# Seven instead of 6.1 conversion steps in every expert slot of an attention and mixture-of-experts kernel

## The chip, the cores and the metric

The kernel runs on one core of a Trainium2 chip. The metric is the device time of one launch in microseconds (us), taken as the median of several runs. The engines are called as in the profile: PE (TensorE, matmuls), ACT (ScalarE), DVE (VectorE), POOL (GpSimd) and SP (SyncE, which issues most of the DMAs). Each engine works through its own queue in program order.

## The reference

```
attn = softmax(scale * q @ k.T + bias(log-distance MLP)) @ v     # 4 x 8 heads, 576 positions, depth 64
x    = attn as [2304 tokens, 512]
e    = argmax(normalised x @ normalised expert_emb)              # 8 experts, one for each token
x    = gate * (relu(x @ w1[e]) @ w2[e])                          # 512 -> 1024 -> 512
out  = (relu(x @ w_in) ** 2) @ w_out                             # 512 -> 2048 -> 512, weights in float64
```

## The kernel before

The program has three stages: the attention, the expert stage and a last dense feed-forward. PE multiplies everything as pairs of 16-bit halves (a high and a low part, three products for each pair), so weights and tokens are split into two halves first.

**Expert stage.** Tokens that share an expert are gathered into slots of 128 rows. `run_slots` (line 1300) runs 22 slots, t = 0 to 21, one after the other. Slot t does, in program order: the first half of the next slot's first product (`ff1(t+1, 0)`), the split of half the first weights of slot t+2 into w1b (`split_w1(t+2, 0)`), the transposition of slot t+2's tokens (`x_T`), the split of slot t+3's tokens (`x_split`), the second half `ff1(t+1, 1)` with `split_w1(t+2, 1)`, the second product `ff2(t)`, its copy-out, and the loads of slot t+4's first weights (`load_slot`). While `ff2(t)` runs, SP issues the four quarters of slot t+1's second weights into the buffers that PE leaves (`load_w2`, line 1020; the profile calls the buffers vt and the source wsc). The weights' loads and splits are conditional: they move data only where a slot's expert differs from that of the slot before. In the traced run that is so for slots 3, 6, 7, 9, 10, 12, 13 and 16.

**The conversion.** Beside this the stage turns the last feed-forward's float64 weights into the halves, in 16 pieces of 1 MB (`convert`, line 1113): pieces 0 to 7 are w_in (into wih, in SBUF), pieces 8 to 15 are w_out (stored to DRAM as wosc). The generator `pieces` cuts the work into 121 steps. Two of them begin it (four loads, L1128 of piece 0), and then come seven for each n from 0 to 16:

```
1  DVE  L1130, L1131 of piece n        (n = 1 to 8: SP also loads piece n+3, L1118 or L1121)
2  ACT  high half of piece n-1         (L1141 or L1152)
3  DVE  L1133 of piece n
4  DVE  low half of piece n-1          (L1143 or L1154; n = 10 to 13: SP also loads piece n+2)
5  DVE  L1135 of piece n
6  POOL L1148 of piece n (w_out only); ACT L1128 of piece n+1
7  SP   store of piece n-1 (w_out only, L1156)
```

Four buffers (wr in the profile) hold raw pieces, two (tb) hold pieces in work. `run_slots` calls `piece(t, n)` at four places of slot t: n = 0 behind `split_w1(t+2, 0)`, n = 1 behind `split_w1(t+2, 1)` and so ahead of `ff2(t)` and its weight loads, n = 2 and n = 3 behind the copy-out of `ff2(t)`. The pace is a constant:

```
def piece(t, n):
    while done[0] < (1 if t < 2 else 1 + (t - 2 + 0.25 * n) * CPACE):
        next(conv, None)
        done[0] += 1
```

At the end of slots 11 to 14 `halves(us, DVE)` and `y_rows` (lines 1050, 1272 and 1274) add the split of four row blocks of the result for the last stage.

**Last stage.** From the end of the slots PE runs the products of the dense feed-forward without a break: `g_unit` (line 1435, weights wih) and `ff2_of` (line 1473, weights woh, loaded from wosc at line 1529).

Of the kernel before, what the change touches and what calls it, by code (L numbers as in the profile page):

```python
# [39 lines left out]
W1S, W2S, YS = 64.0, 64.0, 2.0 ** -8  # L40
WIS, RS, WOS = 64.0, 2.0 ** -8, 64.0
OUTS = 2.0 ** -22
CPACE = 6.1
NCONV, NWIN = 16, 8
HSW = 134
TINY64, HUGE = 2.0 ** -15 * 1.125, 3e38
# [38 lines left out]
def body(ctx: ExitStack, tc: tile.TileContext, q, k, v, wsm, emb, tau, mw1, mw2, win, wout, cst_d, lsk_d, ids_d, out):  # L85
# [873 lines left out]
    with tc.manual_schedule():  # L959
# [331 lines left out]
# [4 lines that stand above are left out]
# [319 lines left out]
```

## Time and profile before

| | |
|---|---|
| runs | 1007.3, 1009.07 and 1011.41 us, median 1009.07 |
| profiled execution | 1002.49 us, span 1000.6 us |
| mean clock granted to TensorE | 0.981 of full speed |
| PE matmuls busy | 945.9 us (95%) |
| DVE, ACT, POOL busy | 652.2, 540.8, 517.8 us (65%, 54%, 52%) |
| slots, first `ff2` to the last stage's first matmul | 398.87 to 642.19 us of the span |

PE is busy nearly all the time, so what counts is where it stands still, in which stage, and what it then waits for. The other engines and the DMA queue matter only where PE waits for them.

### The profile page before, as it was taken

The numbers are of one execution on the slowest core, as the hardware profiler recorded it, in microseconds if no ns is written. First come the engines' busy times: TensorE is split into PE (matmuls) and PEld (weight loads), VectorE is DVE, ScalarE is ACT, GpSimd is POOL, SyncE is SP. The second block draws the span as 40 slices with busy tenths as digits, with TensorE's granted clock in tenths as the row PEclk, the third lists the DMA queues.
The fourth block names the chain that finished last, engine by engine and source line by source line (L and its number), as shares of the span: only waits on it lengthen the run. The fifth ranks groups of instructions, "written<-read, shape, count | busy, mean of one in ns | idle before, by whom it ended". The sixth has DMA issues, their size and how long they took to land. (4 is left out here: it accounts for less than half of the span.)

```text
span 1000.6 us, 25069 instructions
## 1 busy us (share of the span) xinstructions
PE 945.9 (95%) x9725; PEld 750.9 (75%) x9725; DVE 652.2 (65%) x1260; ACT 540.8 (54%) x1000; POOL 517.8 (52%) x509
## 2 busy tenths in 40 slices
PE   8687999999999879999989999999999999999998
PEld 5355676677677658777657766688888888888887
DVE  6665797887988765588966977335455546364442
ACT  5576676877877674456746664355233324324231
POOL 1212548356735362466637787476455645454651
PEclk9799999999999989999999999999999999999999
DMA  8989895998879432698898674371111120111101
GB/s 289 297 259 306 263 302 193 266 293 289 239 248 332 156 132 97 247 340 316 324 407 305 214 296 161 119 315 43 33 54 34 36 59 17 49 44 32 33 1 43
DMA packets 79260, 187.18 MB, mean 187 GB/s; under 512 B 26680, under 2 KB 27320, under 8 KB 76544
## 3 DMA queue, kind: packets, MB, share of 16 engines
q1 hardware_dynamic: 73232, 170.50, 50.8%
q0 software_dynamic: 5904, 15.02, 4.3%
q8 instruction: 78, 1.28, 0.5%
q14 instruction: 46, 0.38, 0.1%
HBM read 171.65 MB, written 51.73 MB: 223 GB/s over the span
## 5 line engine op out<-in xcount | busy, mean ns | idle before, releaser
L1451 POOL TENSOR_TENSOR gf<-gf 128x256 f32<-128x256 f32 x144 | 166.2, 1174 | 144.9 <-DVE gf L1448 124.2
L1435 PE MATMUL pf<-big,wih 128*128 128x256 f16 x1728 | 196.0, 273 | 0.9 <-PEq L1389 0.9
L1435 PEld LDWEIGHTS <-wih 128*128 128x128 f16 x1728 | 169.0, 98 | 20.9 <-issue 1.3
L1473 PEld LDWEIGHTS <-g 128*128 128x128 f16 x1512 | 147.4, 98 | 18.7 <-issue 1.0
L1441 ACT ACTIVATE gf<-pf 128x512 f32<-128x512 f32 x72 | 42.3, 597 | 192.8 <-PE pf L1435 131.4
L475 POOL TENSOR_TENSOR wh<-wr,w2s_c 128x256 f16<-128x256 f32 x128 | 82.9, 679 | 116.6 <-DMA wr<-in_mw_dram 59.3
L1232 PE MATMUL ph<-x,w1b 128*128 128x128 f16 x2112 | 125.1, 219 | 2.5 <-ACT x L1216 1.7
L1232 PEld LDWEIGHTS <-w1b 128*128 128x128 f16 x2112 | 120.5, 98 | 6.9 <-issue 1.9
L1247 PE MATMUL py<-vt,h 128*128 128x512 f16 x528 | 119.2, 383 | 5.7 <-DMA vt<-wsc 5.7
L526 ACT ACTIVATE pr<-ssb,mn 128x576 f32<-128x576 f32 x144 | 111.7, 776 | 8.6 <-DVE mn L513 8.6
L1459 DVE TENSOR_TENSOR g<-gf,g 128x1792 f16<-128x1792 f32 x36 | 85.5, 2375 | 46.5 <-ACT g L1458 46.5
L513 DVE CUSTOM_DVE_ANT_0 ssb<-ps_s,bias 128x576 f32<-128x576 f32 x144 | 107.4, 748 | 6.1 <-DMA bias<-bias_d 5.1
L1448 DVE TENSOR_TENSOR gf<-gf 128x1024 f32<-128x1024 f32 x28 | 34.3, 1225 | 114.2 <-ACT gf L1441 114.2
L502 PE MATMUL ps_s<-kst,qd 128*128 128x288 f16 (+1 forms) x640 | 97.5, 293 | 8.7 <-DVE mn L513 7.2
L1247 PEld LDWEIGHTS <-h 128*128 128x128 f16 x528 | 51.1, 98 | 64.8 <-issue 8.6
L535 PE MATMUL ps_t<-cst,pr 128*128 128x128 f32 x576 | 92.3, 283 | 0.7 <-DVE pt L212 0.4
L560 PE MATMUL pv<-pt,vt 128*64 128x128 f32 (+1 forms) x1280 | 85.7, 277 | 6.8 <-DMA vt<-in_v_dram 5.9
L560 PEld LDWEIGHTS pv<-pt,vt 128*64 128x64 f32 x1280 | 68.0, 142 | 23.7 <-issue 17.3
L535 PEld LDWEIGHTS ps_t<-cst,pr 128*128 128x128 f32 x576 | 64.9, 144 | 23.2 <-issue 19.3
L502 PEld LDWEIGHTS <-qd 128*128 128x128 f16 (+1 forms) x640 | 56.7, 102 | 23.2 <-issue 12.9
L210 ACT COPY pt<-ps_t 128x512 f32<-128x512 f32 x99 | 57.1, 576 | 10.8 <-PE ps_t L535 10.8
L1458 ACT CAST g<-gf 128x1792 f16<-128x1792 f32 x36 | 60.3, 1676 | 4.4 <-POOL gf L1451 4.4
(199 smaller groups left out, 1537.9 us busy)
## 6 DMA issues: line engine op xcount, KB each, us to landing
vt<-wsc SPq DMA_DIRECT2D x88, 512.0 KB
wr<-in_mw_dram SPq DMA_DIRECT2D x76, 512.0 KB
kst<-in_mw_dram SPq DMA_DIRECT2D x44, 512.0 KB
wsc<-wh SPq DMA_DIRECT2D x32, 512.0 KB
bias<-bias_d SPq DMA_DIRECT2D x16, 576.0 KB
bias_d<-rt SPq DMA_DIRECT2D x28, 295.5 KB
qd<-qh SPq DMA_DIRECT2D x64, 128.0 KB
wr<-in_win_dram SPq DMA_DIRECT2D x8, 1024.0 KB
```

The lines of the kernel that those rows point to most:

```text
L475: POOL.tensor_tensor(out=wh[:, 0, n:n + 256], in0=wr[:, n:n + 256], in1=w2s_c.to_broadcast([P, 256]), op=ALU.mult)
L502: PE.matmul(s[r, hf, :288], lhsT=qd[:, h2, i, pr, r], rhs=kst[x - x % 2][:, pr, h2, x % 2, js], start=(i == 0), stop=(i == 1))
L513: DVE.tensor_tensor_reduce(out=ss.rearrange("p (a j) -> p a j", a=2), in0=s[:, :, :288], in1=btile[bkey[u]][:, h2].rearrange("p (a j) -> p ...
L526: ACT.activation(pr_sb[k_ // 2][:, h2], ssb.pop(k_), AF.Exp, bias=mns.pop(k_), scale=-1.0, accum_out=sums[c, b][:, h:h + 1])
L535: PE.transpose(pt_ps[k_][:, jc * P:(jc + 1) * P], src[:, j0:j0 + P], eye)
L560: PE.matmul(pv[o, cs], lhsT=vb[:, 2 * jc + h2, d] if jc < 4 else vb[o, 8, d], rhs=a[h2][:, jc, cs] if jc < 4 else e[o, cs], start=(jc == 0 ...
L1232: PE.matmul(p_[:, f4, :], lhsT=w[:, a, kc, f * P:(f + 1) * P], rhs=x2[:, b, kc, :], start=(i == 0), stop=(i == 11))
L1247: PE.matmul(p_, lhsT=h2[:, a, fc, :], rhs=wb2[fc // 2][:, b, fc % 2, :], start=(i == 0), stop=(i == 23))
L1435: PE.matmul(p_[:, h], lhsT=wih[:, a, kc, f * P:(f + 1) * P], rhs=y2[:, b, kc, :], start=(i == 0), stop=(i == 11))
L1451: POOL.tensor_tensor(out=g[:, d], in0=g[:, x], in1=g[:, y], op=op)
L1459: DVE.tensor_tensor(out=gt[:, 1, :, c:c + 2, :], in0=g[:, 1:8], in1=gt[:, 0, :, c:c + 2, :], op=ALU.subtract)
L1473: PE.matmul(ps, lhsT=gt[:, a, s, c, :], rhs=woh[:, c, b, w, :], start=(i == 0 and first), stop=(i == 23 and end), skip_group_check=True)
```

## The change

The pace of the conversion goes from 6.1 to 7 steps a slot.

```diff
-CPACE = 6.1
+CPACE = 7.0
```

With 7.0 the call at n = 0 of every slot from 3 on runs step 6 of a piece, n = 1 runs steps 7 and 1, and n = 2 and n = 3 together, behind `ff2(t)`, run steps 2 to 5. The last step comes in slot 19, where with 6.1 it comes in slot 21. No instruction's size changes.

SP's queue in slot 6, from the end of `load_slot(9)` over the store of slot 5's rows (y_d) to the first quarter of slot 7's second weights (vt from wsc), before:

```order
L1011 DMA kst_105<-in_mw_dram 128x1024
L1263 DMA y_d<-ys 128x514
L1020 ISA
L1020 DMA vt_106<-wsc_65 128x2048
L1036 UNCONDITIONAL_BRANCH
```

And the same place now:

```order
L1011 DMA kst_105<-in_mw_dram 128x1024
L1263 DMA y_d<-ys 128x514
L1118 DMA wr_7791<-in_win_dram 128x2048
L1036 UNCONDITIONAL_BRANCH
L1020 ISA
L1020 DMA vt_106<-wsc_65 128x2048
```

In each of slots 3 to 10 a conversion load of 1 MB (L1118 or L1121) stands ahead of the slot's weight loads now. Before, the loads of slots 3, 4 and 5 stood behind the second weights and ahead of the first, slot 6 had none, and those of slots 7 to 10 already stood ahead.

DVE's queue at the turn from slot 14 to slot 15, from the second pair of weight splits for slot 16 (L1027) to the low half of slot 16's first hidden rows (the L1238 at the end), before:

```order
L1027 SCALAR_TENSOR_TENSOR w1b<-wr_5262,w1b 128x2x512 x2
L1036 UNCONDITIONAL_BRANCH x2
L1031 TENSOR_LOAD ne_i
L1154 SCALAR_TENSOR_TENSOR wr_8433<-tb,wr_8433 128x1792
L1256 COPY ys<-ga 128x2
L1135 SCALAR_TENSOR_TENSOR tb<-wr_8655,tb 128x1024
L1050 TENSOR_TENSOR xs<-us_78,xs 128x512
L1272 COPY meta<-us_78 128x2
L1274 CAST orow<-us_78 128x1
L1001 SCALAR_TENSOR_TENSOR zid<-ti 128x1
L1002 TENSOR_TENSOR yidx<-yidx,zid 128x1
L1238 SCALAR_TENSOR_TENSOR h_9651<-ph,h_9651 128x512
```

And now, from right behind the same pair of splits:

```order
L1130 TENSOR_SCALAR tb<-tb 128x1024
L1131 TENSOR_SCALAR tb<-tb 128x1024
L1256 COPY ys<-ga 128x2
L1133 SCALAR_TENSOR_TENSOR tb<-wr_9148,tb 128x1024
L1154 SCALAR_TENSOR_TENSOR wr_8665<-tb,wr_8665 128x1792
L1135 SCALAR_TENSOR_TENSOR tb<-wr_9148,tb 128x1024
L1050 TENSOR_TENSOR xs<-us_78,xs 128x512
L1272 COPY meta<-us_78 128x2
L1274 CAST orow<-us_78 128x1
L1001 SCALAR_TENSOR_TENSOR zid<-ti 128x1
L1002 TENSOR_TENSOR yidx<-yidx,zid 128x1
L1238 SCALAR_TENSOR_TENSOR h_9674<-ph,h_9674 128x512
```

All five DVE instructions of a piece stand between the splits and the hidden rows now, where before L1130, L1131 and L1133 stood elsewhere.

## Rows read from the trace of the kernel before

**Rows 1.** Windows: us; PE, PEld, DVE, ACT, POOL busy; clock, DMA share, GB/s

```profile
400.00:642.00 242.00, 233.31 (x2628) 168.94 (x2626) 181.26 (x268) 138.69 (x172) 157.91 (x137) 0.99 0.75 277
...
642.00:998.00 356.00, 354.08 (x3240) 316.36 (x3240) 167.51 (x160) 126.34 (x158) 182.86 (x161) 1.00 0.19 59
```

**Rows 2.** What PE waited for from 395 to 650: us, times, longest

```profile
PE py L1247 <- DMA vt<-wsc: 5.7, 3, 4.2
PE ph L1232 <- ACT x L1216: 1.0, 1, 1.0
PE pf L1435 <- PEq L1389: 0.9, 1, 0.9
PE ph L1232 <- DVE w1b L1027: 0.8, 2, 0.6
PE px L1215 <- POOL xs L1050: 0.4, 1, 0.4
```

**Rows 3.** PE's timeline, slots 6, 7, 10, 16: start, us, what, idle before

```profile
462.10 2.84 PE L1232 MATMUL ph<-x,w1b 128*128 128x128 f16 x48
...
477.29 5.34 PE L1247 MATMUL py<-vt,h 128*128 128x512 f16 x24 [1.35 <-DMA vt<-wsc]
...
514.94 7.03 PE L1247 MATMUL py<-vt,h 128*128 128x512 f16 x24 [4.17 <-DMA vt<-wsc]
...
580.91 2.84 PE L1232 MATMUL ph<-x,w1b 128*128 128x128 f16 x48 [1.04 <-ACT x L1216]
```

**Rows 4.** Windows of the slot stage, columns as in rows 1

```profile
454.00:456.00 2.00, 2.00 (x11) 0.92 (x10) 2.00 (x3) 2.00 (x4) 1.02 (x1) 1.00 0.47 141
456.00:462.00 6.00, 6.00 (x70) 4.34 (x69) 6.00 (x6) 3.05 (x5) 5.76 (x4) 1.00 0.84 300
462.00:478.00 16.00, 14.64 (x185) 11.34 (x183) 11.45 (x19) 10.07 (x13) 8.32 (x7) 1.00 0.99 361
478.00:488.00 10.00, 10.00 (x122) 7.53 (x121) 8.75 (x12) 6.01 (x9) 6.76 (x5) 1.00 1.02 406
488.00:494.00 6.00, 6.00 (x42) 3.16 (x40) 5.78 (x7) 5.97 (x8) 3.41 (x3) 1.00 0.31 82
...
516.00:518.00 2.00, 2.00 (x6) 0.76 (x5) 2.00 (x3) 0.09 (x1) 0.88 (x1) 0.50 1.02 412
```

**Rows 5.** The page's DMA issues: the conversion's loads of pieces 0 to 7

```profile
wr<-in_win_dram SPq DMA_DIRECT2D x8, 1024.0 KB
```

**Rows 6.** SP's timeline, slots 5 and 6: start, us, issues

```profile
455.29 4.22 SPq L1020 DMA_DIRECT2D vt<-wsc  x4
462.07 0.34 SPq L1118 DMA_DIRECT2D wr<-in_win_dram  x1
464.02 2.63 SPq L1011 DMA_DIRECT2D kst<-in_mw_dram  x4
...
467.83 2.74 SPq L1020 DMA_DIRECT2D vt<-wsc  x4
```

**Rows 7.** DVE's timeline, slots 5, 14 and 15: start, us, what

```profile
457.60 3.31 DVE L1027 SCALAR_TENSOR_TENSOR w1b<-kst,w1b 128x1024 f16<-128x1024 f32 x2
460.83 1.21 DVE L1135 SCALAR_TENSOR_TENSOR tb<-wr,tb 128x1024 uint32<-128x1024 uint32 x1
...
564.27 2.34 DVE L1027 SCALAR_TENSOR_TENSOR w1b<-wr,w1b 128x1024 f16<-128x1024 f32 x2
...
571.70 2.01 DVE L1154 SCALAR_TENSOR_TENSOR wr<-tb,wr 128x1792 f16<-128x1792 f32 x1
...
575.51 0.77 DVE L1050 TENSOR_TENSOR xs<-us,xs 128x512 f16<-128x512 f32 x1 [0.59 <-ACT xs L1046]
...
578.17 0.68 DVE L1238 SCALAR_TENSOR_TENSOR h<-ph,h 128x512 f16<-128x512 f32 x1
578.99 0.93 DVE L1130 TENSOR_SCALAR tb<-tb 128x1024 f32<-128x1024 f32 x1
```

**Rows 8.** What SP waited for from 478 to 500: us, times, longest

```profile
SPq L1011 <- DMA wr<-in_win_dram: 2.4, 1, 2.4
```

## The prediction

> **What bounds the kernel now.** I read the busy shares first, then the windows of the two stages that the pace can touch, then what PE waited for there, and last the places of those waits in the timelines.
>
> From 642 us on PE is busy 354.08 of 356 us [rows 1], so a microsecond that the slots lose or win arrives whole at the end, and weights that are ready earlier win nothing there. In the slots PE is busy 233.31 of 242 us [rows 1]. All that the pace can remove is the rest: its waits add up to 8.8 us, of which 5.7 us are for second weights still under way (vt from wsc), and the others are a wait for ACT's copy (1.0), the branch at the end of the stage (0.9), first weights not yet split by DVE (0.8) and tokens not yet split by POOL (0.4) [rows 2]. The weight waits stand ahead of the second products of slots 7 (1.35 us) and 10 (4.17 us), and 0.2 us inside slot 9's [rows 2, 3]. After the 4.17 us the granted clock is 0.50, the lower of TensorE's two levels (1.2 GHz), and the product takes 7.03 us where slot 7's takes 5.34: 1.69 us more. Behind the 1.35 us the clock stays at 1.00 [rows 3, 4].
>
> So two things decide: when the second weights land, and how late DVE (181 of 242 us busy in the stage, and behind it ACT and POOL) is in the slots where weights are split.
>
> **What the change does.** The 121 steps remain, and so do their instructions; they move. Three places matter.
>
> *Loads ahead of slot 7's weights.* A conversion load is 1024 KB [rows 5], 1.05 MB, and the full DMA queue moves 406 GB/s [rows 4], so it takes 2.6 us. Before, slot 5's load was issued at 462.07, behind slot 6's second weights (from 455.29) and ahead of slot 9's first weights (464.02); slot 7's second weights followed at 467.83, and the DMAs were full (share 0.99 from 462 to 478) until PE got them at 477.29 [rows 3, 4, 6]. Now slot 5's load stands ahead of slot 6's weights, some 7 us earlier, and slot 6's load stands where it delays slot 7's. Behind slot 6's weights, slot 7's see the same bytes as before: 2 MB of first weights, a row store, 1 MB of conversion. What can differ is how much of slot 5's load fits ahead. From 454 to 462 the DMAs were idle 0.53 x 2 + 0.16 x 6 = 2.0 us [rows 4]. The load must wait for its buffer, which DVE's L1135 in slot 4 gives back. In the new order that ends near 454.7: behind the pair of splits, whose like in slot 5 end at 460.83, come the steps of one piece, about 5 us (three like L1135 at 1.2 and some 1.4 for L1130 and L1131), and slot 4 is one slot of 11.1 us (243.3 / 22) earlier [rows 7]. So about half of the first 1.06 us of idle is lost to that wait, and 1.5 us are filled. That pushes slot 6's weights, and all behind them, by 2.6 - 1.5 = 1.1 us. SP no longer waits for a buffer between slot 6's and slot 9's weights, which closes the little idle behind 462 (0.01 x 16 = 0.2 us) and perhaps 0.1 us more. I take +0.8 us: slot 7 waits 2.15 us instead of 1.35. The bounds are 0 (all idle filled, 2.6 - 2.0 = 0.6, less what SP saves) and the whole 2.6 us. Slot 6's own product has room: it starts about 464.8 (477.29 less the wait and 11.1), 9.5 us behind the first issue of its weights, and these take 2.6 + 1.3 us now. Slot 6's load waits in the same way for L1135 in slot 5, with slot 7's weights queued behind it on SP; that is due near 466, and the weights were issued at 467.83 before, so up to 1.8 us of lateness costs nothing. The clock: 2.15 us lies nearer to the 1.35 that kept 1.00 than to the 4.17 that lost it, so 0, with 1.69 us as the bound.
>
> The Trainium skill (DMA: Bandwidth & Descriptors, section on queues, rings and completion order) says that on each DMA engine descriptors are consumed in ring order. By that rule alone slot 7's weights are late by the whole load issued ahead of them, +2.6 us, and the sum below would be +2.2 instead of +0.4. The trace so far agrees that order rules (the weights landed behind all that was issued ahead), but also shows the idle share that takes up part of it.
>
> *Slots 8 to 10.* Here one conversion load a slot stood ahead of the weights before and stands there now, so the same bytes lie between slot 7's and slot 10's weights. Both PE and the DMAs are late by the 0.8 us, and the 4.17 us with the 1.69 us behind them stay: 0. The gap in the DMAs (share 0.31 from 488 to 494 [rows 4]) comes from SP, which waited 2.4 us for a 1 MB load to land before it issued on [rows 8]. Slot 7's load is now one place nearer to slot 8's weights; that leaves the wait as it is.
>
> *DVE at slots 14 and 15.* Between the splits for slot 16 and h of slot 16 DVE now has all of a piece, before only its low half and L1135. Ahead of the splits it loses L1133 (1.14 us from start to start, like L1135) and gains a later low half, which waits for ACT: about -0.5 us for the splits' end, 571.7 to 571.2 [rows 7]. From there: L1130 and L1131 1.6 (0.93 and an uncontended 0.7), L1133 1.14, the low half 1.93 (2.01 less the overlap), L1135 1.14, and from L1050 to h the 2.66 us of the row (575.51 to 578.17): 571.2 + 8.5 = 579.7, with h's 0.7 us 580.4, where before it was 578.9 [rows 7]. PE writes that bank again in slot 16 at 580.91 after 1.04 us of waiting for ACT [rows 3]; without that wait, and with 0.5 of the 0.8 us of waiting for the split gone, it could start at 579.4. So it waits 1.0 us, for DVE instead of ACT, and the place gives -0.5 + 0 = -0.5 us, I take -0.4. Bounds: both waits gone, -1.9, or the splits no earlier and h a contended microsecond later, +1.5. ACT's copy is no longer late, because POOL's step now lies a whole second product ahead of the ACT step that needs it. POOL's 0.4 us I leave.
>
> *The store in slot 15* stands ahead of slot 16's second weights. It waits for the low half, done at 575.9 in the sum above; 0.9 MB at 2.3 us and the first quarter at 1.3 land before 582, and the product is due at 586.9 (580.91 and 6 us more of first products). 0.
>
> *Slots 4 and 5* both split. In the second pair, L1135 comes before h where it came behind it: +1.14, against 0.6 us by which slot 4's splits start earlier. Slot 5's end at 460.83, PE reads them from 462.10 [rows 3, 7]: a margin of 1.27 us goes to 0.7. So 0, as for the pairs 7, 8 and 10, 11.
>
> *The end.* The conversion ends in slot 19. Behind it PE waits only at the branch, 0.9 us [rows 2], which stays: 0.
>
> The sum is +0.8 - 0.4 = +0.4 us on the profiled execution, 1002.49 (span 1000.6 and 1.9 around it). That execution lies 0.65% under the median of the runs, 1009.07, so I add the change to the median: 1009.5 us, no difference. From no change a measurement tells about 0.5%, 5 us.
>
> **The rivals.**
>
> *The moved load counts in full (slower, not measurably).* Slot 7's weights come the whole 2.6 us late, PE waits 3.95 us and loses the clock: +2.6 + 1.69 - 0.4 = +3.9, 1013.0 us. For it speaks the full share from 462 on, against it the 2.0 us of idle ahead. Chance 0.15. (It is what the ring order of the Trainium skill's page DMA: Bandwidth & Descriptors would give here, taken alone.)
>
> *DVE becomes the bound in the paired slots (slower).* A slot with splits now holds 4 splits, 5 steps and 2 hidden rows. If DVE's long instructions stretch as the second pair of splits does in slot 5 (3.3 us for two, where slot 14's first pair took 2.3 [rows 7]), the splits of slots 7, 10 and 13 come late. The margin is 0.7 us; with three stretched instructions more in each pair, 2.7 us, PE waits 2.0 us three times: +6.0 + 0.4, 1015.5 us. It decides from 1.6 us of waiting in each pair on. Against it: DVE is busy 75% in the stage. Chance 0.10.
>
> *SP runs freer (faster).* If the earlier load lets SP go on at 488 without the 2.4 us [rows 8], slot 9's and 10's weights are 2.4 us earlier; slot 10 waits 1.8 us and keeps the clock, -2.4 - 1.69, and with slot 7's 1.35 us also gone, -5.4: 1003.7 us. The same order of SP's issues there speaks against it. Chance 0.08.
>
> *The waits of the late slots and of slot 7 vanish by the regular order:* -1.35 - 1.9 - 0.4 = -3.6, 1005.4 us. Chance 0.17.
>
> **The numbers.** The forecast has 0.50 (1007.5 to 1011.5 by itself). Faster by more than 0.5%: the third rival, and a little of the last: 0.09. Slower: the second and a little of the first: 0.12. Within: 0.79. The range takes the first and the last rival with 1.5 us for the scatter of the runs: 1004 to 1014.5.
>
> **What would show it.** Right: slot 7's second product waits about 2.2 us at full clock, slot 10's about 4.2 us with 1.7 us of slow clock, the wait for ACT in slot 16 is one for DVE, and the slots from the first `ff2` to the last stage take 243.3 us within 1.5. Wrong: slot 10's wait changes by more than 1 us, PE waits for w1b (L1027) in slots 6, 9 or 12, or a wait of several us for POOL's tokens appears in slots 13 to 18.

## The result, and the profile after

The changed kernel is slower: 1025.48 us against 1009.33 us (medians of six runs each), a ratio of 1.0129 with a 95% interval from 1.0097 to 1.0162. The forecast was 1009.5, no difference. The profiled execution took 1018.58 us, its span is 1016.4 us, 15.8 us more than before.

First what PE waited for in the slots (which engine and tile, for what; us, times, longest), the answer to [rows 2]:

```profile
PE px L1215 <- POOL xs L1050: 13.3, 4, 6.2
PE py L1247 <- DMA vt<-wsc: 4.8, 3, 3.7
PE ph L1232 <- issue: 1.3, 3, 0.5
PE pf L1435 <- PEq L1389: 1.0, 1, 1.0
```

The wait for second weights has become a little shorter, those for ACT's copy and for DVE's split are gone, and a wait for POOL's tokens has come that was 0.4 us. PE's timeline (start, us, what, idle before) shows where, with the second product of slot 0 as the first row and the first matmul of the last stage as the last:

```profile
400.73 5.34 PE L1247 MATMUL py<-vt,h 128*128 128x512 f16 x24
...
480.16 2.75 PE L1247 MATMUL py<-vt,h 128*128 128x512 f16 x12 [0.57 <-DMA vt<-wsc]
...
483.46 2.75 PE L1247 MATMUL py<-vt,h 128*128 128x512 f16 x12 [0.55 <-DMA vt<-wsc]
...
517.89 7.03 PE L1247 MATMUL py<-vt,h 128*128 128x512 f16 x24 [3.69 <-DMA vt<-wsc]
...
545.05 0.61 PE L1215 MATMUL px<-eye,xs 128*128 128x128 f16 x4 [6.24 <-POOL xs L1050]
545.45 4.39 PE L1232 MATMUL ph<-x,w1b 128*128 128x128 f16 x48
...
583.19 0.40 PE L1215 MATMUL px<-eye,xs 128*128 128x128 f16 x4 [1.95 <-POOL xs L1050]
...
597.05 0.40 PE L1215 MATMUL px<-eye,xs 128*128 128x128 f16 x4 [2.26 <-POOL xs L1050]
...
611.02 0.40 PE L1215 MATMUL px<-eye,xs 128*128 128x128 f16 x4 [2.81 <-POOL xs L1050]
...
657.94 2.23 PE L1435 MATMUL pf<-big,wih 128*128 128x256 f16 x19 [0.96 <-PEq L1389]
```

The four waits stand in the middle of `x_T` in slots 12, 15, 16 and 17, ahead of the low halves that POOL makes (the expectations below count the last three as slots 14 to 16, one too low). After the longest the granted clock is 0.63 on the average of the next first product (window 545.5 to 549.8), so TensorE spent most of it at the lower of its two levels, and the product takes 4.39 us where the others take 2.84. From the first second product to the last stage the slots now take 657.94 - 400.73 = 257.2 us, before 243.3: 13.9 us more. Of these, tokens make 13.3 - 0.4 = 12.9, the slow clock 1.55, gaps with no releaser in slot 3 1.3, second weights 4.8 - 5.7 = -0.9, and the waits for ACT and DVE that are gone -1.0 and -0.8: 13.05 of 13.9. The other 1.9 us of the span lie ahead of the slots. So the question is POOL.

POOL's timeline of before, slots 10 to 12 (the subtractions of step 6 are L1148, the token split L1049 and L1050, the row write L1265):

```profile
527.76 1.81 POOL L1265 DMA_INDIRECT y_d<-ys,yidx  x1 [10.89 <-DVE w1b L1027]
...
533.27 1.16 POOL L1050 TENSOR_TENSOR xs<-xg,xs 128x512 f16<-128x512 f32 x1
...
541.71 2.01 POOL L1050 TENSOR_TENSOR xs<-xg,xs 128x512 f16<-128x512 f32 x1
...
544.32 1.09 POOL L1265 DMA_INDIRECT y_d<-ys,yidx  x1 [0.47 <-DVE ys L1256]
545.44 2.90 POOL L1148 TENSOR_TENSOR tb<-tb 128x256 f32<-128x256 f32 x4
```

And of the changed kernel:

```profile
530.22 1.62 POOL L1265 DMA_INDIRECT y_d<-ys,yidx  x1 [9.80 <-DMA wr<-in_mw_dram]
...
534.54 5.65 POOL L1148 TENSOR_TENSOR tb<-tb 128x256 f32<-128x256 f32 x4
540.17 1.73 POOL L1049 TENSOR_SCALAR xg<-xg 128x512 f32<-128x512 f32 x1
541.99 3.01 POOL L1050 TENSOR_TENSOR xs<-xg,xs 128x512 f16<-128x512 f32 x1
```

Both kernels hold POOL still for some 10 us at a row write in slot 10. (The releasers beside it, DVE and a weight load, are not the cause: the write waits for the reads of finished rows. In e2 below, with these reads a slot earlier, the wait stands in slot 9 with 7.4 us, and in e5 it is gone.) Before, slot 11 then had only its token split, and the first subtractions came in slot 12 behind everything else. Now they come in slot 11, ahead of the split, and take 5.65 us instead of 2.90. The low half is done at 545.0, and that is when PE goes on. The windows from 530 to 624 us (columns as in [rows 1]) say how full POOL is from there; before first, then after:

```profile
530.00:624.00 94.00, 91.71 (x1064) 67.68 (x1063) 73.17 (x90) 55.73 (x68) 77.15 (x68) 1.00 0.70 251
```

```profile
530.00:624.00 94.00, 80.74 (x926) 60.22 (x923) 76.15 (x87) 54.61 (x66) 87.62 (x69) 0.96 0.63 234
```

POOL, the last of the busy times, goes from 77.15 to 87.62 of 94 us; over 242 us of slots it had been 157.91 [rows 1], 65%, which hid this stretch. In the changed kernel's timeline no gap of POOL between 530.2 and 630 us is over 0.33 us; it waits 0.3 us for DVE there and for no other engine.

### The profile page after: what moved, and what is told of

Same layout as the page of the kernel before. It is cut to its first block, busy times and chain, and to the rows that moved or that the text cites. A ratio compares the mean times of both kernels' runs of the same rounds, so it can differ in the third digit from the quotient of the medians.

```text
span 1016.4 us, 25073 instructions
## 1 busy us (share of the span) xinstructions
PE 949.9 (93%) x9725; PEld 752.1 (74%) x9725; DVE 655.5 (64%) x1260; ACT 540.3 (53%) x1000; POOL 523.0 (51%) x509
## 5 line engine op out<-in xcount | busy, mean ns | idle before, releaser
L475 POOL TENSOR_TENSOR wh<-wr,w2s_c 128x256 f16<-128x256 f32 x128 | 86.4, 705 | 113.7 <-DMA wr<-in_mw_dram 51.1
L502 PE MATMUL ps_s<-kst,qd 128*128 128x288 f16 (+1 forms) x640 | 97.6, 294 | 11.4 <-DVE mn L513 5.6
L1448 DVE TENSOR_TENSOR gf<-gf 128x1024 f32<-128x1024 f32 x28 | 34.3, 1225 | 114.2 <-ACT gf L1441 114.2
L210 ACT COPY pt<-ps_t 128x512 f32<-128x512 f32 x99 | 57.2, 577 | 16.8 <-PE ps_t L535 10.2
```

Of the source, the lines that this page charges most:

```text
L475: POOL.tensor_tensor(out=wh[:, 0, n:n + 256], in0=wr[:, n:n + 256], in1=w2s_c.to_broadcast([P, 256]), op=ALU.mult)
L502: PE.matmul(s[r, hf, :288], lhsT=qd[:, h2, i, pr, r], rhs=kst[x - x % 2][:, pr, h2, x % 2, js], start=(i == 0), stop=(i == 1))
```

## The experiments

The table has one row for each kernel: its ratio to the kernel before, run on the same chip, with the 95% interval; then, from its one profiled execution, PE's waits for tokens and for second weights, and the slots' length from the first second product to the last stage's first matmul. The length doesn't hold the part ahead of the slots, which begins them anywhere from 398 to 412 us in these profiles.

| kernel | ratio | tokens | weights | slots |
|---|---|---|---|---|
| before | 1 | 0.4 | 5.7 | 243.3 |
| changed | 1.0129 [1.0097, 1.0162] | 13.3 | 4.8 | 257.2 |
| e1 subtractions behind the split | 1.0213 [1.0164, 1.0261] | 0 | 4.9 | 264.7 |
| e2 reads at slot 8 | 1.0057 [1.0026, 1.0089] | 7.2 | 5.3 | 253.5 |
| e3 all one slot later | 1.0110 [1.0056, 1.0164] | 10.7 | 5.0 | 256.6 |
| e4 loads behind the weights | 1.0146 [1.0087, 1.0205] | 14.0 | 1.0 | 258.2 |
| e5 reads at slot 5 | 1.0101 [1.0064, 1.0138] | 7.5 | 6.2 | 256.3 |
| e6 no subtractions | 0.9981 [0.9957, 1.0005] | 0.4 | 3.8 | 240.4 |
| e8 = e4 + e5 | 1.0062 [1.0037, 1.0087] | 7.7 | 5.4 | 254.5 |
| e16 copy on ACT | 1.0080 [1.0052, 1.0108] | 6.7 | 4.8 | 249.4 |
| e12 = e4 + e16 | 1.0043 [0.9993, 1.0094] | 10.0 | 3.2 | 251.1 |
| e14 = e3 + e12 | 1.0016 [0.9986, 1.0047] | 5.6 | 1.4 | 245.9 |
| e10 before, pace 7 from slot 12 | 1.0169 [1.0122, 1.0216] | 9.4 | 5.2 | 265.2 |
| e11 before, subtractions twice | 1.0298 [1.0247, 1.0349] | 6.3 | 4.6 | 270.1 |
| e7 before, e4 + e5 | 0.9999 [0.9973, 1.0024] | 0.3 | 5.0 | 246.7 |
| e9 before, e4 | 0.9965 [0.9928, 1.0002] | 2.7 | 3.3 | 245.2 |
| e13 before, e12 | 0.9985 [0.9955, 1.0015] | 4.1 | 1.8 | 243.2 |

### The first theory: the subtractions' place

The after trace suggested the order in POOL's queue. Four edits of the changed kernel were to tell it from the others. e1 hands the subtractions to a list and runs them behind `x_split` and `y_out` of the same slot, and moves nothing else:

```diff
+        pq = []
+        pool_step = lambda: [pq.pop(0)() for _ in pq[:]]
...
-            for d, x, y, op in ((4, 0, 1, ALU.subtract), (5, 2, 4, ALU.subtract), (6, 2, 0, ALU.subtract),
-                                (7, 3, 5, ALU.subtract)):
-                POOL.tensor_tensor(out=tb[:, d], in0=tb[:, x], in1=tb[:, y], op=op)
+            subs = (4, 0, 1), (5, 2, 4), (6, 2, 0), (7, 3, 5)
+            pq.append(lambda: [
+                POOL.tensor_tensor(out=tb[:, d], in0=tb[:, x], in1=tb[:, y], op=ALU.subtract) for d, x, y in subs])
...
-                y_out()
+                y_out(), pool_step()
```

> Only POOL's four subtractions of step 6 (L1148) move: behind x_split and y_out of the same slot, all else as in the changed kernel. Theory (POOL's order: the subtractions stand ahead of the token split that PE needs next): PE's waits for POOL's tokens fall from 13.3 us to under 1, the slow clock behind the longest (1.6 us) goes with them, and the time falls by 13 to 15 us, from 1025 to about 1011. Rival 1 (POOL is full: with one piece in every slot from 11 on its work is longer than a slot, wherever it stands): the waits only move, the time falls by less than 4 us. Rival 2 (the conversion loads ahead of the second weights): POOL's order is beside the point, no change.

The waits for tokens are gone, and the kernel is no faster: 1.0213 where the change alone is 1.0129, slots of 264.7 us. The theory falls. Who waited for whom from 500 to 650 us, on ACT and POOL:

```profile
ACT wr L1152 <- POOL tb L1148: 47.4, 8, 8.0
...
POOL xg L1049 <- ACT xs L1048: 31.7, 7, 5.7
```

Both engines now wait, for each other. POOL's timeline in slots 15 and 16, and under it ACT's:

```profile
599.18 3.03 POOL L1148 TENSOR_TENSOR tb<-tb 128x256 f32<-128x256 f32 x4
...
608.80 0.69 POOL L1049 TENSOR_SCALAR xg<-xg 128x512 f32<-128x512 f32 x1 [5.37 <-ACT xs L1048]
...
612.99 3.04 POOL L1148 TENSOR_TENSOR tb<-tb 128x256 f32<-128x256 f32 x4
```

```profile
602.25 1.70 ACT L1152 ACTIVATE wr<-tb 128x1792 f16<-128x1792 f32 x1 [5.55 <-POOL tb L1148]
...
607.97 0.72 ACT L1048 ACTIVATE xs<-xg 128x512 f16<-128x512 f32 x1
```

It is a circle. ACT's conversion (L1152) waits for the subtractions, ACT's half of the next token split (L1048) stands behind it in ACT's queue, POOL's half waits for that, and the next subtractions stand behind POOL's half. One turn is 612.99 - 599.18 = 13.8 us, and with one piece in each slot the slot can't be shorter. With the subtractions ahead of the split (the change) the circle doesn't close: from 530 to 632 us POOL has no wait for ACT, and PE pays by waiting for tokens instead.

e2 issues the four reads of finished rows, for which POOL's row write in slot 10 waits, a slot earlier; e3 puts the whole conversion a slot later; e4 issues the conversion's load and store behind the second weights:

```diff
-                    if t == 9:
+                    if t == 8:
```

> The four reads of finished rows (L1374) are issued at the end of slot 8 and not of slot 9, so that POOL's write of rows that waits for them (9.8 us) comes a slot earlier. Theory, if POOL comes late to slot 11's step because of that wait: the longest wait of PE for tokens, 6.2 us in slot 12, falls under 1 with its 1.6 us of slow clock, and the three of 2.0 to 2.8 us in slots 14 to 16 go too if they are what POOL carries on: -7.5 to -14.5 us, 1018 to 1011. If the order alone makes them, all four stay and the time is 1025. Rival 2 (loads): no change but what the reads do to the DMA queue, within 2 us.

```diff
-            while done[0] < (1 if t < 2 else 1 + (t - 2 + 0.25 * n) * CPACE):
+            while done[0] < (1 if t < 3 else 1 + (t - 3 + 0.25 * n) * CPACE):
```

> The pace of 7 and every step's place in a slot stay, but the whole conversion runs one slot later, so the first w_out piece's step 6 is in slot 12. Theory (POOL's order): slots 13 to 16 keep their waits of 2 to 3 us each where weights are split, the 6.2 us of slot 12 shrink since POOL has a slot without step 6 behind its 9.8 us: 1016 to 1021. Rival 1 (POOL full): about the same as 1025, less one slot's excess, 1022. Rival 2 (loads ahead of the second weights): waits for second weights move, the tokens' waits are no part of it: 1025 within 2.

```diff
                     more(t)
-                    piece(t, 1)
                 ff2(t, hi)
+                if first: piece(t, 1)
```

> Only SP's order moves: the conversion load and store of steps 1 and 7 are issued behind the second weights of the next slot (behind ff2) and not ahead. Theory (POOL's order): PE's 13.3 us for tokens stay; of the 4.8 us for second weights (3.7 in slot 10, with 1.7 us of slow clock) up to 5 go: 1020 to 1025. Rival 2 (loads): the time goes back to 1009 or below, and the waits for tokens vanish with the loads. Rival 1: 1020 to 1025 like the theory.

e2 took the first wait away, and only that. Its two large waits for tokens:

```profile
579.89 0.61 PE L1215 MATMUL px<-eye,xs 128*128 128x128 f16 x4 [3.74 <-POOL xs L1050]
...
607.14 0.61 PE L1215 MATMUL px<-eye,xs 128*128 128x128 f16 x4 [2.80 <-POOL xs L1050]
```

They stand in slots 15 and 17, two of 0.4 and 0.3 us beside them in 14 and 16; slot 12 has none. So the 6.2 us there come from POOL's 10 us of lateness, and the 1.95 + 2.26 + 2.81 = 7.0 us of the later slots are 7.2 us without it. The slots got only 3.8 us shorter. Slot 10's wait for second weights (4.47 us instead of 3.69) and the product behind it (8.08 instead of 7.03) take 1.8 us more, and the clock now falls behind two waits where it fell behind one: from the second product of slot 14 to that of slot 15 pass 16.8 us, 1.6 more than the wait and a slot's 11.4. e3 shortened the tokens' waits to 10.7 us, the one behind the lateness to 3.3, as expected; its ratio can't be told from the change's. e4 took the waits for second weights from 4.8 to 1.0 us and left the tokens (14.0) and the time where they were: the loads are not the cause. What their place wins is lost again, most of it because the clock now falls behind three waits for tokens (first products of 4.48, 4.46 and 4.19 us instead of 2.84) where it fell behind one.

### The second theory: POOL is late, or has too much

If only the lateness counted, a change without it would be free. e5 has `if t == 5:` in the place of e2's 8, so that the reads are through before POOL's first row write. e6 leaves the subtractions out. e8 is e4 and e5 together, e7 the same two edits on the kernel before.

> The changed kernel with the four reads of finished rows at the end of slot 5, before POOL's first write of rows (slot 8), so that no write waits for them. Second theory (POOL comes 9 to 10 us late into slot 11 because of that wait, and one piece a slot leaves it no time to catch up, whatever the order): no wait of PE for tokens over 1 us, 13 to 15 us less than the changed kernel, 1009 to 1012. Rival 1 (POOL is full in slots with splits, with or without the lateness): the waits of 2 to 3 us in slots 14 to 16 stay, 1016 to 1018. Rival 2 (place alone: the subtractions ahead of the split): as rival 1 in the time, with a wait in each slot from 11 to 16.

```diff
-            for d, x, y, op in ((4, 0, 1, ALU.subtract), (5, 2, 4, ALU.subtract), (6, 2, 0, ALU.subtract),
-                                (7, 3, 5, ALU.subtract)):
+            for d, x, y, op in (
+                                ):
                 POOL.tensor_tensor(out=tb[:, d], in0=tb[:, x], in1=tb[:, y], op=op)
```

> POOL's four subtractions of step 6 are left out (so the halves of w_out are not those of the reference); loads, DVE and ACT steps stay at a pace of 7. Second theory: everything that the change costs runs over POOL's subtractions, so PE's waits for tokens go and the time is that of the kernel before or up to 3 us under it, 1005 to 1010. If loads or DVE's new places cost something of their own, the time stays over 1012.

> The kernel before (6.1), with the reads at the end of slot 5 and the conversion's loads and stores behind the second weights of the next slot. Theory: POOL's wait of 10.9 us goes, which cost PE next to nothing before (0.4 us of tokens, 1.0 of ACT), and of the 5.7 us for second weights and 1.7 us of slow clock some 5 go: 1003 to 1006. If second weights are late because of the first weights and not of the conversion's loads, 1008 to 1010.

> The changed kernel (7.0) with both: reads at the end of slot 5, loads behind the second weights. Second theory: no lateness of POOL, so the regular order costs nothing, and the second weights' 4.8 us and the slow clock go too: 1003 to 1006, like the kernel before with the same two edits. Rival 1 (POOL full): 3 to 9 us over the kernel before with the same edits.

e6 settles which part of the change costs: without the subtractions, and with every load, DVE and ACT step at its new place, the time is that of before (0.9981) and the slots are 240.4 us, 2.9 less. e5 refutes "late and nothing else": no row write waits for the reads, yet 7.5 us for tokens remain, all from slot 15 on. Its time gained less than the tokens did, since the reads at slot 5 delay slot 7's second weights (one wait of 4.2 us, with the slow clock behind it); the same in e7 (5.0 us) and e8 (4.4 us), so the times that I had expected of these two were wrong. Between e8 and e7, which differ in the pace alone, lie 1017.17 - 1009.05 = 8.1 us, within the 3 to 9 of the rival that POOL is full. POOL's timeline in e5, from one piece's subtractions to the next, shows no gap over 0.34 us:

```profile
550.90 3.27 POOL L1148 TENSOR_TENSOR tb<-tb 128x256 f32<-128x256 f32 x4 [0.34 <-DVE tb L1135]
554.16 0.69 POOL L1049 TENSOR_SCALAR xg<-xg 128x512 f32<-128x512 f32 x1
554.93 1.59 POOL L1050 TENSOR_TENSOR xs<-xg,xs 128x512 f16<-128x512 f32 x1
556.47 0.65 POOL L1057 COPY ga<-xg 128x2 f32<-128x2 f32 x1
557.28 2.01 POOL L1265 DMA_INDIRECT y_d<-ys,yidx  x1 [0.17 <-issue]
559.60 1.61 POOL L985 DMA_INDIRECT ti<-id_d,xidx  x1 [0.31 <-issue]
561.51 1.39 POOL L996 DMA_INDIRECT xg<-x_d,ti  x1 [0.31 <-issue]
562.92 2.91 POOL L1148 TENSOR_TENSOR tb<-tb 128x256 f32<-128x256 f32 x4
...
576.37 5.34 POOL L1148 TENSOR_TENSOR tb<-tb 128x256 f32<-128x256 f32 x4
...
591.55 3.80 POOL L1148 TENSOR_TENSOR tb<-tb 128x256 f32<-128x256 f32 x4
```

The three turns take 12.0, 13.45 and 15.2 us. A slot of PE without waits, products and token transposes together, is 11.4 us (561.11 to 572.54 in the changed kernel's trace). So POOL falls behind by 0.6 to 3.8 us a slot, whether or not it starts late.

### The third theory: one piece a slot is too much for POOL and what it feeds

e9 is e4's edit on the kernel before. e10 keeps the kernel before up to slot 12 and has a pace of 7 from there, with the subtractions behind `x_split` and `y_out` in every slot. e11 does each subtraction twice in the kernel before. e12 is the changed kernel with e4's edit and with a small copy of `x_split` on ACT:

```diff
-            while done[0] < (1 if t < 2 else 1 + (t - 2 + 0.25 * n) * CPACE):
+            while done[0] < (1 if t < 2 else 1 + max((t - 2 + 0.25 * n) * CPACE, (t - 2 + 0.25 * n) * 7 - 8.75)):
```

> The kernel before up to slot 12, and a pace of 7 from there: one w_out piece in every slot from 12 to 19, but its subtractions in the second quarter of the slot, behind x_split and y_out, never ahead of them. Theory as it stands (one piece a slot is more than POOL and what waits for it can do, wherever the subtractions stand): PE waits 6 to 12 us in slots 13 to 17 for ACT, DVE or tokens, 1016 to 1022. Place alone (only subtractions ahead of the split cost): no such waits, 1007 to 1011.

```diff
-                                (7, 3, 5, ALU.subtract)):
+                                (7, 3, 5, ALU.subtract)) * 2:
```

> The kernel before with each of the four subtractions done twice: POOL has 2.9 to 5 us more for each piece. Theory (POOL is nearly full at 6.1 already): its piece of 12 to 15 us grows to 15 to 18, over the 13.1 us that a piece has at 6.1 (7/6.1 of a slot of 11.4), PE waits 2 to 4 us a piece in the pieces with splits and the time rises by 12 to 25 us, 1021 to 1034. If POOL had room at 6.1: under 3 us more.

```diff
-            POOL.tensor_copy(ga[t], a[:, DM:XW])
+            ACT.copy(ga[t], a[:, DM:XW])
```

> The changed kernel with the loads behind the second weights, and with the small copy of x_split (L1057, 128x2, 0.6 to 2.0 us on POOL in each slot) on ACT. Theory (POOL full): a slot's work on POOL gets 0.7 to 2 us shorter, PE's waits for tokens fall from 14.0 us (loads behind, copy on POOL) to 2 to 7, and the time from 1020 to 1008 to 1014. If the subtractions' place alone made the waits, they stay within 3 us, 1018 to 1021.

> The kernel before (6.1) with the conversion's loads and stores behind the second weights alone, the reads back at slot 9. In the changed kernel that edit took the waits for second weights from 4.8 to 1.0 us. If the loads ahead of them make those waits: 5.7 us become about 1.5 and the 1.7 us of slow clock go, -5 to -6 us, 1003 to 1005. If other bytes make them, no change, 1008 to 1011.

All three tests of the theory moved the time its way: e12 (1010.98 us) into the range named, e10 (1024.32) and e11 (1037.87) past theirs. e10 costs as much as the change (1.0169) though no subtractions stand ahead of a split. It is e1's circle again: ACT waits for the subtractions, 51.5 us in eight waits, and POOL for ACT's half of the token split, 27.0 us from 500 to 645. So e10 shows that one piece a slot costs in this order too, not that POOL by itself is full; that is shown by the rows of e5 and of the changed kernel, where POOL has no such waits.

e11 adds 26.8 us to the slots, a little more than expected: POOL, and ACT that waits for it (28.7 us), had no room for them at 6.1 either. e12 has 7.1 us less in the slots than e4, from a copy of two numbers a row whose like in before took 1114 ns on the average of the eight from 530 to 640 us and up to 1.98 us. Its waits for tokens fell to 10.0 us only, not to 2 to 7: 6.0 are those of slot 12, behind the lateness, and 4.0 the later ones, 8.0 in e4. e16 has the copy on ACT and nothing else, e14 all three reliefs (a slot later, loads behind, copy on ACT), e13 the last two on the kernel before:

> The changed kernel with nothing but x_split's small copy (L1057) moved from POOL to ACT; loads ahead of the second weights as in the changed kernel. Theory (a slot's work on POOL is too long): PE's 13.3 us for tokens fall to 5 to 10, the time to 1012 to 1018, half or more of the change's cost back. If the copy counted for nothing and the loads' place made the gain of the kernel with both: 1022 to 1027.

> The changed kernel (7.0) with the whole conversion one slot later, loads behind the second weights and the copy on ACT. Theory: the one-slot delay lets POOL catch up from its wait of 10 us before the first subtractions, the copy makes a slot's work on POOL fit; of the 10.0 us for tokens left without the delay (6.0 of them in slot 12) 2 to 5 remain, 1003 to 1008, level with the kernel before or a little under it. If place or pace still cost with POOL relieved, 1010 or more.

> The kernel before (6.1) with the loads behind the second weights and with x_split's small copy (L1057) on ACT. Theory (POOL nearly full, second weights late through the conversion's loads): with loads behind alone PE still waited 2.7 us for tokens, 3.3 for second weights and 2.1 for ACT; the copy takes 0.6 to 2 us a slot off POOL, so the 2.7 and part of the 2.1 go: 2 to 4 us under that kernel, 1000 to 1003. If the copy on ACT delays ACT's other work instead: 1004 to 1008.

e16: tokens 6.7 us (4.3 in slot 12, 2.4 later), slots 7.8 us shorter, 1.0080 where the change is 1.0129; so the copy made e12's gain and the loads' place none. e14: 1.0016 [0.9986, 1.0047]. With POOL relieved the pace of 7 costs nothing that can be measured, and wins nothing; the 5.6 us for tokens that are left, and the median of 1012.32 us (1010.5 for the kernel before beside it), are above what I had expected. e13 and e9 on the kernel before can't be told from it either (0.9985, 0.9965), and their slots, 243.2 and 245.2 us, are no shorter than its 243.3: no version tried here beats the kernel before. Two expectations failed there. In e9 3.3 us for second weights were left where 1.5 were expected, and the 5 to 6 us didn't come. In e13 the tokens, which were to go, rose from 2.7 to 4.1 us, 3.0 of them in slot 12, behind a row write for which POOL stood still for 11.4 us; the copy doesn't shorten that lateness.

### Why the same four subtractions take 2.9 or 5.65 us

> None of the reference's work: POOL's subtraction (128x256, 32-bit) 16 times by itself, then 16 times beside each of DVE's split (two operands, 16-bit result), DVE's bit step (two 32-bit operands), DVE's one-operand step, and ACT's copy; and DVE's three by themselves. If the two engines hold each other up, as the four subtractions of 5.65 us beside DVE's splits and 2.9 us elsewhere suggest: 0.7 us by itself and 1.2 to 1.5 beside the two-operand steps, 0.7 beside ACT. If POOL's long rows had another cause (start delays, memory): 0.7 in every stretch.

The stretches of this first measurement ran into each other, since nothing tied POOL's instructions to DVE's; two rows of it stand in the last section. The second one parts the stretches with a pair of copies:

> The first measurement of POOL's subtraction beside DVE ran its stretches into each other; here a pair of small copies parts them. None of the reference's work. By the rows of the first one: 0.69 us by itself and beside ACT; beside DVE's two-operand steps either POOL is stretched (1.2 to 1.6 us, DVE's step 1.7) or DVE stands still while POOL's row of steps runs on (POOL 0.69, one DVE step 4 to 9 us). If they do not hold each other up: 0.69 and 1.14 in every stretch. Beside DVE's one-operand step: 0.69 if only two-operand steps take the shared way, 1.2 if all do.

Its groups (busy us, mean ns of one). L112 is POOL's subtraction by itself, L120 the same beside DVE's split (L118; beside the bit step it is 1587 ns too), L136 beside DVE's one-operand step (L134), L141 beside ACT; L115 and L131 are DVE's split and one-operand step by themselves:

```profile
L118 DVE SCALAR_TENSOR_TENSOR wl<-wa,wh 128x1024 f16<-128x1024 f32 x16 | 25.6, 1602 | 0.5
...
L120 POOL TENSOR_TENSOR tb<-tb 128x256 f32<-128x256 f32 x16 | 25.4, 1587 | 1.4 <-DVE tb L103 0.3
...
L134 DVE TENSOR_SCALAR wu<-wa 128x1024 f32<-128x1024 f32 x24 | 23.1, 961 | 0.8
L115 DVE SCALAR_TENSOR_TENSOR wl<-wa,wh 128x1024 f16<-128x1024 f32 x16 | 19.6, 1225 | 0.5
...
L136 POOL TENSOR_TENSOR tb<-tb 128x256 f32<-128x256 f32 x16 | 16.9, 1054 | 1.4 <-DVE tb L103 0.3
L131 DVE TENSOR_SCALAR wu<-wa 128x1024 f32<-128x1024 f32 x24 | 16.6, 694 | 0.8
L141 POOL TENSOR_TENSOR tb<-tb 128x256 f32<-128x256 f32 x16 | 11.6, 727 | 1.4 <-DVE tb L103 0.3
L112 POOL TENSOR_TENSOR tb<-tb 128x256 f32<-128x256 f32 x16 | 11.6, 724 | 5.9 <-DVE tb L103 4.7
```

Four subtractions are 4 x 0.72 = 2.9 us by themselves and beside ACT, and 4 x 1.59 = 6.3 us beside DVE's two-operand steps; the 5.65 us of the changed kernel lie between. DVE pays too, 1602 instead of 1225 ns. So in slots where DVE splits weights, POOL's work gets longer just where it has no time to spare. The Trainium skill (SBUF — State Buffer, section on who interferes with whom) says that a DVE instruction with two SBUF inputs contends with a GpSimd instruction that reads SBUF. These rows agree.

## Why the prediction was wrong

The step that failed is "POOL's 0.4 us I leave", with the half sentence ahead of it: ACT's copy "is no longer late, because POOL's step now lies a whole second product ahead of the ACT step that needs it". It asked who needs the subtractions and not what stands behind them in POOL's queue, nor how long a slot's work on POOL is. What the runs showed in its place: PE waits 13.3 us for tokens, and the cost runs over the subtractions (shown by e6). Three things make it up. One piece in every slot, where before a slot had 6.1 / 7 of one, takes POOL's work to 12 to 15 us in a slot of 11.4 (shown by e5's rows; e11, e12 and e16 lengthen or shorten that work, and the time follows): 7.0 us of the tokens. POOL comes 10 us late into slot 11, where the first piece now stands: 6.2 us and the 1.55 of slow clock (e2 and e5 moved the reads ahead, and slot 12's wait was gone). And the subtractions stretch beside DVE's steps (measured by e17). Between the two places tried, ahead of the split and behind it, the place only decides who waits: PE for tokens, or ACT for the subtractions (e1, e10).

The sizes could have been read before. POOL's busy time of 157.91 of 242 us stood in [rows 1], and I took no window of POOL for the slots that the change fills.

- *Slot 7's second weights:* forecast +0.8 us, measured 0.57 + 0.55 = 1.12 instead of 1.35, at a granted clock of 1.00 (478 to 484 us). The sign was wrong: -0.2 us lies just outside the bounds of 0 and 2.6. Order counts there, as e4 shows (4.8 to 1.0 us over all), and as the Trainium skill's ring order (DMA: Bandwidth & Descriptors, section on queues, rings and completion order) says; but the 2.6 us that the prediction made of that rule alone didn't come.
- *Slot 10:* 3.69 us and a product of 7.03, forecast 4.17 and 7.03 [rows 3]: right within the 1 us named.
- *DVE in slots 14 and 15:* the waits for ACT and for split weights went, and none for DVE came. That isn't proof in the changed kernel, where PE itself was late. In e6, where it wasn't, all of these waits are gone too, so as far as a kernel without the subtractions can show it, the bound of -1.9 us was right and not the -0.4 taken.
- *The store, slots 4 and 5, the end:* no wait came at the first two, and 1.0 instead of 0.9 us at the end, as forecast.
- *The rivals:* none had POOL in it. DVE as the bound came nearest in size (1015.5), but PE waits for no split; and its 2.7 us don't follow from the rows it names, by which three stretched instructions cost 3 x (3.3 - 2.3) / 2 = 1.5 us. "The late-slot waits vanish", 1005.4, comes near what e6 shows without the subtractions: its slots are 2.9 us shorter, where that rival had 3.6, though its time (0.9981) can't be told from that of before.
- *What was to show it wrong:* the last sign on that list, tokens in slots 13 to 18, is the one that came, in slots 15 to 17; the longest wait came in slot 12, a slot earlier than I had it.

Still open: how much of the 7.0 us the stretching beside DVE makes; no run parts it from the number of pieces. The changed kernel's trace bounds it: with each of POOL's groups of a turn at the shortest that it shows from 530 to 632 us (L1148 2.89, L1049 0.69, L1050 1.16, L1057 0.19, L1265 1.07, L985 1.05, L996 1.00) and 0.8 us of gaps, a turn would be 8.9 us by estimate and fit into a slot of 11.4, where the five turns from 534.54 to 602.36 take 11.7 to 15.8. By that estimate one piece a slot is too much only with the instructions that take longer than their shortest, and of these only the subtraction was measured beside DVE. The gaps of 1.3 us in slot 3 are in e6 as well, and 0.9 us of the kind in e9 at a pace of 6.1; their cause was not looked for.

## What to carry to other kernels

When a step moves to an earlier place, look at every in-order queue that it enters: add up what that engine has to do in one period there, from the rows of that stretch and not from its share of the whole stage, and compare it with the period of the engine that bounds. An engine that is idle a third of the time can be full for 100 us, and if a loop of waits closes over two engines (here POOL's subtractions, ACT's conversion, the next token split), the turn of the loop bounds the period even with both idle. The two orders tried here only chose who waits; taking work off the full engine, here a copy of two columns, is what gave time back.

## What the runs showed of the hardware beyond that

POOL and DVE hold each other up step by step, yet by less than whole instructions: 16 subtractions and 16 splits side by side are through in 26.7 us (42.66 to 69.39). One after the other they are 12.8 and 20.1, 32.9 us; these are the rows of e17's timeline:

```profile
9.01 12.76 POOL L112 TENSOR_TENSOR tb<-tb 128x256 f32<-128x256 f32 x16 [4.69 <-DVE tb L103]
...
22.12 20.11 DVE L115 SCALAR_TENSOR_TENSOR wl<-wa,wh 128x1024 f16<-128x1024 f32 x16
...
42.66 26.16 DVE L118 SCALAR_TENSOR_TENSOR wl<-wa,wh 128x1024 f16<-128x1024 f32 x16
42.82 26.57 POOL L120 TENSOR_TENSOR tb<-tb 128x256 f32<-128x256 f32 x16 [0.27 <-DVE tb L103]
```

In e15 it went otherwise five times: a row of subtractions ran at its full speed of 0.69 us each, and one DVE step that stood beside it took 4.2 to 8.7 us. The longest, with eleven subtractions:

```profile
45.10 8.70 DVE L122 SCALAR_TENSOR_TENSOR wl<-wa,wh 128x1024 f16<-128x1024 f32 x1
45.18 7.55 POOL L143 TENSOR_TENSOR tb<-tb 128x256 f32<-128x256 f32 x11
```

What decides between the two was not settled. DVE's one-operand 32-bit step stretches POOL as well, to 1054 ns, and itself from 694 to 961 on the average of 24 steps, the last of which ran behind POOL's row.
